# Score products on 64 lanes: two heads side by side instead of a stacked 128-lane product, with four score banks, one result bank and row groups of two and four

## The chip, the cores and the metric

One core of a Trainium2 chip runs the whole program. The metric is the device time of one execution in microseconds (us), lower is better.

## The reference

Two attentions follow each other, for batch 4, 768 rows and heads of 64. The first has 8 heads; each row sees the 128 rows up to itself and the first four rows (sinks). Its output x (768 x 512 a batch) goes into a mixture of 4 experts, each a causal attention of its own, of which every row takes two:

```python
keep = is_sink | in_window                       # first stage, 8 heads
x = softmax(where(keep, q @ k.T / 8, -1e9)) @ v  # -> (B, 768, 512)
logits = x @ w_gate                              # second stage, 4 experts
for e in range(4):
    a = softmax(where(causal, -1e9, (x @ wq[e]) @ (x @ wk[e]).T / 8))
    out += (top-2 weight of e) * (a @ (x @ wv[e]) @ wo[e])
```

## The kernel before

Heads go in pairs, since two heads of 64 fill the 128 lanes: four first-stage pairs a batch (`first`) and two second-stage pairs of experts (`second`), 24 units in all. A unit works through six blocks of 128 rows. Each block takes these steps:

- score products on PE into a PSUM bank `s` (L437);
- DVE adds the mask and takes the row's extreme (L638 in the first stage, L578 in the second);
- ACT takes the exponential and its sum (L643, L588);
- DVE and POOL make the factor and scale `p` (L477, L478, L668, L595; in the first stage POOL also merges two blocks, L661);
- PE transposes `p` into `t` (L495, L519), ACT or DVE copies that to `pt` (L339, L341);
- PE multiplies `pt` with the values into a result bank `acc` (L470), each head into its own 64 columns of the array ("cols").

After three blocks the result is read twice, by ACT (L322, high part) and then DVE (L327, low part), into `x` or `y`. Numbers are kept as a high and a low part, so that a product is three: high-high, high-low, low-high. The second stage makes its values (`values`, L772) and its queries and keys (L746) from `x`, and the output (`store`, L817) from `y`.

Score products stand in two forms. In batch 0 the first stage is **flat**: queries and keys hold high and low parts of both heads on 128 lanes, a head on 64 lanes each; three products, head by head alternating, on 64 rows of the array ("rows"). Everywhere else they are **stacked**: the low part of a head is moved by a DMA (L423) into the 64 lanes of the other head, below the high part, so that one 128-lane product with `ks` makes two of the three, and a second one with `kz` (half of it zeros, set once at L274) the third. For that ACT writes the high part twice (L400, 768 columns), DVE writes the low part to `ql` or `kl` (L404), and SyncE issues six DMAs a pair.

The order of work is made by a planner, `Plan`. Each step has a priority (its due time), a cost per engine and the steps and buffers that it waits for. `emit` takes, again and again, the step that can start first, the lower priority first among equals; on PE a step in another mode than the last (full height, "rows", "cols") counts as `STAY` later. A ring gives the number of buffers of a tile: three `s`, three `t`, two `acc`, together the eight PSUM banks. The units follow the list at L832 and L833: in each batch two first-stage pairs, both second-stage pairs of the batch before ("p"), two first-stage pairs.

Of the kernel before, what the change touches and what calls it, by code (L numbers as in the profile page):

```python
# [26 lines left out]
SWITCH = {("full", "cols"): 105, ("cols", "full"): 150, ("full", "rows"): 236, ("cols", "rows"): 236,  # L27
          ("rows", "full"): 90, ("rows", "cols"): 90}

STAY = 9.08  # L30
# [31 lines left out]
class Plan:  # L62
# [7 lines left out]
    def step(self, prio, cost, fn, after=(), new=(), use=(), fifo=None, moves=0, mode="full", behind=()):  # L70
        after = list(after)
        if fifo is not None:
            if fifo in self.fifo:
                after.append(self.fifo[fifo])
        s = Step(prio, cost, fn, after, new, use, moves, mode, behind)
        if fifo is not None:
            self.fifo[fifo] = s
        self.steps.append(s)
        return s

    def emit(self):
        free = {PE: 2000.0, DVE: 5000.0, ACT: 2000.0, POOL: 9500.0, SP: 650.0}
# [63 lines left out]
def kernel(  # L146
# [38 lines left out]
    pools = {tag: ctx.enter_context(tc.tile_pool(name=tag + "_", bufs=n, **(  # L185
        {"space": bass.MemoryType.PSUM} if tag in ("s", "t", "acc") else {}))) for tag, n in rings.items() if tag not in ("kz", "st", "psk", "vs")}
# [84 lines left out]
    kz = [consts.tile([128, 2, NB * SW], F32R, name=f"kz{n}") for n in range(rings["kz"])]  # L271
    for t in kz:
        for e in range(2):
            nc.vector.memset(t[64 - e * 64:128 - e * 64, e, :].bitcast(F32), 0.0)  # L274
    zeroed = itertools.cycle(kz)


    W, W_READY = {}, {}

    def weight(name, n, pieces, prio):  # L280
        cols = (EP if name == "wo" else NCH) * n
        st = buf("v2", [128, NB * E * D])
# [4 lines left out]
        def load():  # L287
            for sl, src in pieces:
                nc.sync.dma_start(sl(st.t[:, :cols].rearrange("p (c n) -> p c n", n=n)), src)

        ld = plan.step(prio, {SP: 460 * len(pieces)}, load, new=[st], fifo="v2", moves=730 * len(pieces))
        W_READY[name] = []
        for a in range(0, cols, 260):
            cs = slice(a, min(a + 260, cols))
            h = plan.step(prio + 3, {ACT: 320}, lambda cs=cs: nc.scalar.activation(hi[:, cs], st.t[:, cs], AF.Copy),
                          after=[ld], use=[st])
            W_READY[name].append(plan.step(
                prio + 3, {POOL: 695},
                lambda cs=cs: nc.gpsimd.tensor_sub(lo[:, cs], st.t[:, cs], hi[:, cs].bitcast(F32)),
                after=[h], use=[st]))  # L300

    def expert_pieces(w):
        return [((lambda t, e=e: t[:, :, e * D:(e + 1) * D]), w[e].rearrange("(c p) d -> p c d", p=128))
                for e in range(E)]
# [40 lines left out]
    class Pair:  # L345


        def __init__(self, ext, flat=False):
            self.ext, self.flat = ext, flat
            self.kw = SW if ext else 128  # L350
            self.n = NB * self.kw - (4 if ext else 0)
            self.qs, self.ks = buf("qs", [128, 2, S], F32R), buf("ks", [128, 2, NB * SW], F32R)
            if not flat:
                self.ql, self.kl = buf("ql", [128, S], F32R), buf("kl", [128, NB * SW], F32R)
                self.kz = Buf("kz", lambda: next(zeroed))
            self.splits = {0: [], 1: []}
            self.ready = {0: [], 1: []}

        def tiles(self, which):
            if self.flat:  # L360
                return [self.ks if which else self.qs]
            return [self.ks, self.kl, self.kz] if which else [self.qs, self.ql]

        def put(self, which, g, ps, t, prio, mul, after):
            use = [t, *self.tiles(which)]
            high, low = [], []  # L370
            w = NB * self.kw
            if which == 0:
                cs = slice(g * 384, g * 384 + 384)
                if self.flat:
                    high.append((ps, lambda: self.qs.t[:, 0, cs]))
                else:
                    high.append((lambda: ps()[:, None, :].to_broadcast([128, 2, 384]), lambda: self.qs.t[:, :, cs]))
                low.append((ps, lambda: self.qs.t[:, 0, cs], lambda: self.qs.t[:, 1, cs] if self.flat else self.ql.t[:, cs]))
            else:
                for sinks in range(2 if self.ext and g == 0 else 1):  # L380
                    js, cs = (slice(0, NB - 1), slice(128, SW)) if sinks else (slice(3 * g, 3 * g + 3), slice(0, 128))

                    def src(sinks=sinks):
                        x = ps()
                        return (x[:, None, :4].to_broadcast([128, NB - 1, 4]) if sinks
                                else x.rearrange("p (j c) -> p j c", c=128))

                    def at(x, js=js, cs=cs):
                        return x.rearrange("p (j c) -> p j c", c=self.kw)[:, js, cs]
                    if self.flat or sinks:  # L390
                        high += [(src, lambda e=e, at=at: at(self.ks.t[:, e, :w])) for e in range(1 if self.flat else 2)]
                    else:
                        high.append((lambda src=src: src()[:, None].to_broadcast([128, 2, 3, 128]),
                                     lambda js=js, cs=cs: self.ks.t[:, :, :w].rearrange("p e (j c) -> p e j c", c=self.kw)[:, :, js, cs]))
                    low.append((src, lambda at=at: at(self.ks.t[:, 0, :w]),
                                lambda at=at: at(self.ks.t[:, 1, :w] if self.flat else self.kl.t[:, :w])))

            def act():
                for src, dst in high:
                    nc.scalar.activation(dst(), src(), AF.Copy, scale=mul)  # L400

            def dve():
                for src, hi, dst in low:
                    nc.vector.scalar_tensor_tensor(dst(), src(), mul, hi().bitcast(F32), op0=OP.mult, op1=OP.subtract)  # L404
            some = 70 if self.ext and which and g == 0 else 0
            h = plan.step(prio, {ACT: some + 380 if self.flat else 2 * some + 690}, act, after, (), use)
            lo = plan.step(prio, {DVE: some * 1.3 + 470}, dve, [h], (), use)
            self.splits[which] += [h, lo]
            if g and not self.flat:
                self.stack(which, prio)  # L410

        def stack(self, which, prio):
            n = self.n if which else S
            for e in range(2):
                s, o = slice(e * 64, e * 64 + 64), slice(64 - e * 64, 128 - e * 64)
                if which:
                    moves = ((lambda e=e, o=o: self.ks.t[o, e, :n], lambda e=e, s=s: self.ks.t[s, e, :n]),
                             (lambda e=e, s=s: self.kz.t[s, e, :n], lambda s=s: self.kl.t[s, :n]))
                else:
                    moves = ((lambda e=e, o=o: self.qs.t[o, e, :n], lambda s=s: self.ql.t[s, :n]),)  # L420
                for dst, src in moves:
                    def go(dst=dst, src=src):
                        nc.sync.dma_start(dst().bitcast(F32), src().bitcast(F32))  # L423
                    self.ready[which].append(plan.step(prio, {SP: 600}, go, self.splits[which], (), self.tiles(which),
                                                       moves=830))

        def scores(self, outs, i, ks):

            qs = slice(i * 128, i * 128 + 128)
            for n in range(3 if self.flat else 2):  # L430
                for o, e in outs:
                    if self.flat:
                        hs, (a, b) = slice(e * 64, e * 64 + 64), THREE[n]
                        lhs, rhs = self.qs.t[hs, a, qs], self.ks.t[hs, b, ks]
                    else:
# [467 lines left out]
```

## Time and profile before

| what | value |
|---|---|
| median of 3 runs | 457.13 us (457.12 to 459.96) |
| the profiled execution | 457.69 us, span 456.0 us, granted clock 0.996 |
| instructions | 11,781, of them 3,920 matmuls |
| DMA | 95,852 packets, 51.94 MB |

Times in a view of the trace are counted from the span's start. The rows of a timeline have start, length, engine, line, operation, tiles, the part of the array (64*128 is half of its rows, 128*64 half of its columns), and the shape; a matmul's end is modelled, and its start is measured. Idle time before an instruction stands in brackets, with what ended it.

### The profile page before, as it was taken

The page shows a single profiled execution, that of the slowest core. Times are in us where ns is not written, and L with a number is a line of the kernel's source. Part 1 is how long each engine was busy: PE and PEld are TensorE (multiplying, and loading weights), DVE is VectorE, ACT ScalarE, POOL GpSimd, SP SyncE. Part 2 cuts the span into 40 slices and gives each one's busy share as a digit, 9 for nine tenths or more (in the row PEclk, how much of TensorE's full clock was granted, in tenths as well). Part 3 has the DMA queues.
Part 4 walks back from the last instruction along what each step waited for, and adds up shares of the span by engine and source line. Part 5 has one row for each costly group of instructions (what it writes and reads, how often), then busy time and mean ns, then how long its engine had stood idle before and what let it go on. Part 6 is the DMA issues. An engine that isn't in the chain of part 4 may idle for free.

```text
span 456.0 us, 11781 instructions
## 1 busy us (share of the span) xinstructions
PE 440.7 (97%) x3920; PEld 390.3 (86%) x3920; DVE 330.3 (72%) x1309; ACT 316.7 (69%) x906; POOL 265.3 (58%) x469
## 2 busy tenths in 40 slices
PE   5998899999999999999999999999999999999996
PEld 4777689999978889999987888999997888998775
DVE  6788783776898786766788788558689875376773
ACT  4898895765798877836688879647589845257540
POOL 7799786545666477435556675363565842025660
PEclk9999899999999999999999999999999999999999
DMA  8997895314466966402477579321413520404012
GB/s 173 199 197 149 208 198 108 81 36 104 85 147 157 220 182 159 106 15 57 105 175 162 130 190 237 73 52 36 105 37 74 128 94 25 105 2 104 2 47 92
DMA packets 95852, 51.94 MB, mean 114 GB/s; under 512 B 84784, under 2 KB 84784, under 8 KB 95792
## 3 DMA queue, kind: packets, MB, share of 16 engines
q1 hardware_dynamic: 95792, 51.19, 48.3%
q8 instruction: 31, 0.51, 0.5%
q14 instruction: 29, 0.24, 0.2%
HBM read 21.05 MB, written 6.29 MB: 60 GB/s over the span
## 4 chain that ended last, share of the span: by engine, by line
PE 81%; ACT 10%; DVE 3%; POOL 2%; issue 2%; DMA 0%; ACTq 0%; POOLq 0%; DVEq 0%
PE acc L470 19%; PE s L437 17%; PE t L746 15%; PE t L495 10%; PE t L772 7%; PE t L817 7%; PE t L720 3%; ACT p L643 2%; ACT pt L339 2%; PE t L519 2%; ACT p L588 2%; ACT ks L400 2%; ACT qs L400 2%; DVE pt L522 1%; PE t L525 1%
## 5 line engine op out<-in xcount | busy, mean ns | idle before, releaser
L437 PE MATMUL s<-ks,qs 64*128 64x260 f32 (+6 forms) x416 | 108.8, 346 | 1.8 <-DVE st L578 0.8
L643 ACT ACTIVATE p<-p,st 128x260 f32<-128x260 f32 (+1 forms) x192 | 93.4, 493 | 10.0 <-DVE st L638 8.7
L668 POOL TENSOR_TENSOR p<-p,st 128x256 f32<-128x256 f32 x96 | 65.5, 686 | 43.2 <-DVE st L478 33.2
L595 POOL TENSOR_TENSOR p<-p,st 128x128 f32<-128x128 f32 (+5 forms) x96 | 87.6, 933 | 3.8
L588 ACT ACTIVATE p<-p,st 128x256 f32<-128x256 f32 (+5 forms) x96 | 64.1, 670 | 28.5 <-DVE st L578 23.8
L638 DVE CUSTOM_DVE_ANT_0 p<-s,bmask 128x260 f32<-128x260 f32 (+1 forms) x192 | 72.2, 399 | 10.9 <-PE s L437 9.4
L437 PEld LDWEIGHTS s<-ks,qs 128*128 128x128 f32 (+1 forms) x416 | 64.5, 198 | 17.3 <-issue 7.1
L339 ACT ACTIVATE pt<-t 128x512 f32<-128x512 f32 (+1 forms) x109 | 57.6, 530 | 30.6 <-PE t L495 21.9
L437 PE MATMUL s<-kz,qs 128*128 128x260 f32 (+4 forms) x272 | 78.3, 304 | 0.0
L495 PE MATMUL t<-ident,p 128*128 128x128 f32 x432 | 63.1, 278 | 2.9 <-ACT qs L400 1.3
L661 POOL TENSOR_TENSOR p<-p 128x256 f32<-128x256 f32 x64 | 46.9, 733 | 18.2 <-ACT p L643 14.5
L495 PEld LDWEIGHTS t<-ident,p 128*128 128x128 f32 x432 | 48.9, 141 | 9.6 <-issue 2.8
L400 ACT ACTIVATE ks<-t 128x768 fp32r<-128x768 f32 (+2 forms) x76 | 38.8, 554 | 23.3 <-PE t L746 16.5
L481 POOL TENSOR_TENSOR st<-st,gate 128x2 f32<-128x2 f32 x48 | 9.4, 195 | 76.8 <-DVE st L478 62.3
L578 DVE CUSTOM_DVE_ANT_0 p<-s,cmask 128x512 f32<-128x512 f32 (+3 forms) x96 | 52.0, 551 | 1.1 <-PE s L437 0.8
L437 PEld LDWEIGHTS s<-kz,qs 128*128 128x128 f32 x272 | 51.6, 190 | 1.4
L400 ACT ACTIVATE qs<-t 128x768 fp32r<-128x768 f32 (+1 forms) x48 | 36.4, 759 | 13.6 <-PE t L746 10.3
L470 PE MATMUL acc<-pt,v 128*64 128x128 f32 x672 | 43.6, 277 | 0.4
L470 PEld LDWEIGHTS acc<-pt,v 128*64 128x64 f32 x672 | 36.0, 137 | 6.7 <-issue 2.6
L470 PE MATMUL acc<-pt,vn 128*64 128x128 f32 x448 | 40.3, 283 | 1.0 <-ACT pt L339 0.8
L618 POOL TENSOR_TENSOR dv<-vn 128x256 f32<-128x256 f32 x32 | 22.8, 731 | 29.9 <-PE acc L470 29.9
L341 DVE COPY pt<-t 128x512 f32<-128x512 f32 (+1 forms) x51 | 33.0, 647 | 9.7 <-PE t L495 9.1
(101 smaller groups left out, 959.6 us busy)
## 6 DMA issues: line engine op xcount, KB each, us to landing
qs<-ql SPq DMA_DIRECT2D x40, 192.0 KB, 3.1
vn<-in_v_dram SPq DMA_DIRECT2D x32, 192.0 KB, 3.4
out_dram<-o SPq DMA_DIRECT2D x24, 256.0 KB, 3.8
qn<-in_q_dram SPq DMA_DIRECT2D x30, 192.0 KB, 3.6
kn<-in_k_dram SPq DMA_DIRECT2D x30, 192.0 KB, 3.9
ks<-ks SPq DMA_DIRECT2D x24, 197.0 KB, 4.1
kz<-kl SPq DMA_DIRECT2D x24, 197.0 KB, 4.2
ks<-ks SPq DMA_DIRECT2D x16, 192.0 KB, 3.4
```

The lines of the kernel that those rows point to most:

```text
L339: nc.scalar.activation(dst(), src(), AF.Copy)
L400: nc.scalar.activation(dst(), src(), AF.Copy, scale=mul)
L437: nc.tensor.matmul(o, lhs, rhs, start=n == 0, stop=n == (2 if self.flat else 1))
L470: nc.tensor.matmul(o if e is None else o[e * 64:e * 64 + 64], lhs, rhs, start=first and e is not None, stop=last and i % 3 == 2)
L495: nc.tensor.transpose(t.t[:, 2 * e + c, :], block(e, c), ident)
L578: nc.vector.tensor_tensor_reduce(out=p.t[:, cs], in0=s.t[:, :(c1 - c0) * 128], in1=mask[:, cs], scale=1.0, scalar=st.t[:, 3, es] if c0 els ...
L588: nc.scalar.activation(x, x, AF.Exp, bias=st.t[:, 0, es], scale=-1.0, accum_out=st.t[:, 1, es])
L595: nc.gpsimd.tensor_mul(x, x, st.t[:, 2, e:e + 1].to_broadcast([128, n * 128]))
L638: nc.vector.tensor_tensor_reduce(out=p.t[:, e, a:], in0=s.t[:, a:RW], in1=row_mask[i][:, a:], scale=1.0, scalar=BIG, op0=OP.add, op1=OP.mi ...
L643: nc.scalar.activation(x, x, AF.Exp, bias=st.t[:, 0, e:e + 1], scale=-1.0, accum_out=st.t[:, 1, e:e + 1])
L668: nc.gpsimd.tensor_mul(x, x, st.t[:, 2, :][:, :, None].to_broadcast([128, 2, z - a]))
L746: nc.tensor.matmul(ps, w[a][:, c, es], X[b, c].t[:, x, cs], start=c == 0 and n == 0, stop=c == NCH - 1 and n == 2)
```

## The change

All score products become flat, in both stages: six matmuls a step, the two heads in turn. `ql`, `kl`, `kz`, the double write on ACT, the zeroing and all stacking DMAs go. A step takes two score banks at once, one a head; the ring `s` grows from three to four and `acc` shrinks from two to one. The row blocks of a unit form the groups 0-1 and 2-5 in place of 0-2 and 3-5: a group's result is one read of 256 or 512 columns, the second stage's queries and keys are made by group, and its steps wait only for the group they need. `wo` is loaded in two pieces into the ring `o` in place of one into `v2`. The planner's constants are new, among them the due times of the weights (`WP`, `WS`: from 7 to 15 apart), and so is the order of units: in a batch 0, 1, p0, 2, p1, 3, in the last 0, 1, 2, p0, 3, p1, c0, c1. The list is now kept in priority order per ring (`fifo`). Code for parts of batch 0 is there but off (`PARTS = 0`).

```diff
-STAY = 9.08
+STAY = 15.87
-    rings = {"qn": 2, "kn": 2, "vn": 3, "ql": 1, "kl": 1, "qs": 2, "ks": 2, "kz": 2, "x": 6,
-             "v2": 1, "y0": 1, "y1": 1, "p": 6, "dv": 2, "pt": 6, "psk": 4, "sk": 2, "vs": 2, "o": 2,
-             "gate": 2, "gates": 1, "st": 6, "s": 3, "t": 3, "acc": 2}
+    rings = {"qn": 2, "kn": 2, "vn": 3, "qs": 3, "ks": 3, "x": 6,
+             "v2": 1, "y0": 1, "y1": 1, "p": 8, "dv": 2, "pt": 6, "psk": 4, "sk": 2, "vs": 2, "o": 2,
+             "gate": 2, "gates": 1, "st": 6, "s": 4, "t": 3, "acc": 1}
...
-        def stack(self, which, prio):
...
-                    def go(dst=dst, src=src):
-                        nc.sync.dma_start(dst().bitcast(F32), src().bitcast(F32))
...
-            for n in range(3 if self.flat else 2):
-                for o, e in outs:
-                    if self.flat:
-                        hs, (a, b) = slice(e * 64, e * 64 + 64), THREE[n]
-                        lhs, rhs = self.qs.t[hs, a, qs], self.ks.t[hs, b, ks]
-                    else:
-                        lhs, rhs = self.qs.t[:, e, qs], (self.kz if n else self.ks).t[:, e, ks]
-                    nc.tensor.matmul(o, lhs, rhs, start=n == 0, stop=n == (2 if self.flat else 1))
+            for n, (a, b) in enumerate(THREE):
+                for e, o in enumerate(outs):
+                    hs = slice(e * 64, e * 64 + 64)
+                    nc.tensor.matmul(o, self.qs.t[hs, a, qs], self.ks.t[hs, b, ks], start=n == 0, stop=n == 2)
...
-            for heads in pair.heads():
-                for c0 in range(0, n, 4):
-                    c1 = min(c0 + 4, n)
-                    ss = {e: buf("s", [128, 512]) for e in heads}
+            for c0 in range(0, n, 4):
+                c1 = min(c0 + 4, n)
+                ss = [buf("s", [128, 512]) for _ in range(2)]
...
-            for g in range(2):
-                cs = slice(g * 384, g * 384 + 384)
+            for lo, hi in groups:
+                cs, n = slice(lo * 128, hi * 128), (hi - lo) * 128
...
-    ORD = "0 1 p0 p1 2 3"
-    LAST = "0 1 p0 p1 2 3 c0 c1"
+    CUTS_0, CUTS_N = "0 2 6", "0 2 6"
...
+    ORD = "0 1 p0 2 p1 3"
+    LAST = "0 1 2 p0 3 p1 c0 c1"
-    WP, WS = 2.88, 7.16
+    WP, WS, LOAD_0, PREP_3, VALUES_0 = 6.25, 14.87, 16.82, 11.14, 16.87
```

Three places on PE show how the order changes. The first is in the last two units of the program, where the score steps of a second-stage pair (s<-ks,qs) stand between transposes (t<-ident,p) and result products (acc<-pt,v). Before:

```order
L495 MATMUL t<-ident,p 128x128 x10
L470 MATMUL acc<-pt,v_6219 64x128 x10
L437 MATMUL s<-ks,qs 128x384
L437 MATMUL s<-kz_207,qs 128x384
L495 MATMUL t<-ident,p 128x128 x14
L470 MATMUL acc<-pt,v_6219 64x128 x14
L437 MATMUL s<-ks,qs 128x512
```

and now (line 416 is the score product, 466 the transpose, 437 the result product):

```order
L437 MATMUL acc<-pt,v_6295 64x128 x14
L466 MATMUL t<-ident,p 128x128 x10
L416 MATMUL s<-ks,qs 128x384 x6
L466 MATMUL t<-ident,p 128x128 x12
L437 MATMUL acc<-pt,v_6295 64x128 x22
L416 MATMUL s<-ks,qs 128x512 x12
L466 MATMUL t<-ident,p 128x128 x12
```

A head's two stacked products could stand alone, in the same mode as the transposes; now a step is six products of both heads in a mode of its own, often two steps together (x12).

The second place is the change from one result bank to the next, in the last unit. Before (the numbers are those of the tiles):

```order
L470 MATMUL acc_6564<-pt_6645,v2_6219 64x128 x4
L470 MATMUL acc_6564<-pt_6652,v2_6219 64x128 x4
L470 MATMUL acc_6564<-pt_6660,v2_6219 64x128 x4
L470 MATMUL acc_6689<-pt_6667,v2_6219 64x128 x2
L437 MATMUL s_6695<-ks_6409,qs_6328 128x512
```

and now, where the row of x4 is the last product of one result and the row of x6 begins the next:

```order
L437 MATMUL acc<-pt,v_6295 64x128 x4
L416 MATMUL s<-ks,qs 128x512 x6
L416 MATMUL s<-ks,qs 128x256 x6
L437 MATMUL acc<-pt,v_6295 64x128 x6
L805 MATMUL t<-woh,y_6584 128x512
```

Before, the next result began right behind the last, in the other bank; now other work stands between them while the one bank is read.

The third place is the end of the program, from the last transposes on. Before:

```order
L470 MATMUL acc<-pt,v_6219 64x128 x8
L495 MATMUL t<-ident,p 128x128 x14
L470 MATMUL acc<-pt,v_6219 64x128 x14
L817 MATMUL t<-woh,y_6524 128x512
L817 MATMUL t<-wol,y_6524 128x512
```

and now:

```order
L437 MATMUL acc<-pt,v_6295 64x128 x10
L466 MATMUL t<-ident,p 128x128 x12
L437 MATMUL acc<-pt,v_6295 64x128 x12
L805 MATMUL t<-woh,y_6584 128x512
L805 MATMUL t<-wol,y_6584 128x512
```

In both, four stores follow the last result product. Before, the first of the four is row block 2, of the group 0-2; now all four are of the group 2-5.

More of the change, by code (lines that the diff above doesn't have):

```diff
@@ L81, in emit @@
     def emit(self):
+        for line in self.fifo.values():
+            line.sort(key=lambda s: s.prio)
+            for a, b in zip(line, line[1:]):
+                if a not in b.after:
+                    b.after.append(a)
+                    a.then.append(b)
+                    b.waiting += 1
         free = {PE: 2000.0, DVE: 5000.0, ACT: 2000.0, POOL: 9500.0, SP: 650.0}
@@ L455, in mode, with fresh, tile, k_at @@
-        def mode(self):
-            return "rows" if self.flat else "full"
+        def fresh(self, which):
+            return ([], [self.tile(which)]) if self.ready[which] else ([self.tile(which)], [])
+        def tile(self, which):
+            return self.ks if which else self.qs
+        def k_at(self, x, js, cs):
+            x = x[..., :self.nk * self.kw]
+            return x.rearrange("p (j c) -> p j c" if len(x.shape) == 2 else "p e (j c) -> p e j c", c=self.kw)[
+                ..., js.start - self.k0:js.stop - self.k0, cs]
@@ L458, with score_cost, __init__ @@
+    def score_cost(n):
+        return 22 + 3 * max(109, n / 2.4 + 14)
     class Acc:
-        def __init__(self):
+        def __init__(self, lo, hi):
             self.b = buf("acc", [128, 512])
+            self.lo, self.hi = lo, hi
             self.begun, self.steps = set(), []
         def add(self, i, e, lhs, rhs, last=False):
-            o = self.b.t[:, (i % 3) * 128:(i % 3) * 128 + 128]
-            first = e not in self.begun
+            o = self.b.t[:, (i - self.lo) * 128:(i - self.lo) * 128 + 128]
+            nc.tensor.matmul(o[e * 64:e * 64 + 64], lhs, rhs, start=e not in self.begun, stop=last and i == self.hi - 1)
@@ L469, in add, with bufs @@
             self.begun.add(e)
-            nc.tensor.matmul(o if e is None else o[e * 64:e * 64 + 64], lhs, rhs,
-                             start=first and e is not None, stop=last and i % 3 == 2)
+        def bufs(self):
+            return ([], [self.b]) if self.steps else ([self.b], [])
     def factor(prio, st, after, weight=None, weight_after=()):
@@ L528, in av @@
         def av():
-            for r, acc in enumerate(accs):
+            for r in range(2):
                 for c in range(3):
@@ L535, in av, with wide_rows @@
                             acc.add(i + r, e, diff[0](i + r, e) if c else value[0](i + r - 1, e), (part if c else whole).t[:, r, e, :])
-        new = [] if accs[1].steps else [accs[1].b]
-        both = list({id(x): x for x in accs}.values())
-        s = plan.step(prio + AV_LAG, {PE: 1308}, av, [moved, tri, moved_sk, made_vs] + value[1] + diff[1], new,
-                      [whole, part, sk, vs] + value[2] + diff[2] + [acc.b for acc in both if acc.b not in new],
-                      fifo="av", mode="cols")
-        for acc in both:
-            acc.steps.append(s)
-    def wide_rows(prio0, step, pair, blocks, masks, value, weights, finish):
-        acc = None
+        new, used = acc.bufs()
+        acc.steps.append(plan.step(prio + AV_LAG, {PE: 1308}, av, [moved, tri, moved_sk, made_vs] + value[1](None) + diff[1], new,
+                                   [whole, part, sk, vs] + value[2] + diff[2] + used, fifo="av", mode="cols"))
+    def wide_rows(prio_of, pair, blocks, masks, value, weights, finish, groups):
         for i in range(NB):
-            if i % 3 == 0:
-                acc = Acc()
-            prio = prio0 + step * i
+            lo, hi = next(g for g in groups if g[0] <= i < g[1])
+            if i == lo:
+                acc = Acc(lo, hi)
+            prio = prio_of(i)
             cols, mask = blocks[i], masks[i]
@@ L591, in wide_rows, with exp @@
+            for e in range(2):
+                def exp(p=ps[e], es=slice(e, e + 1), n=n, st=st):
+                    x = p.t[:, :n * 128]
+                    nc.scalar.activation(x, x, AF.Exp, bias=st.t[:, 0, es], scale=-1.0, accum_out=st.t[:, 1, es])
+                sums.append(plan.step(prio - WIDE_E, {ACT: 278 + 0.833 * 128 * n}, exp, prev[e], (), [ps[e], st]))
+            r = factor(prio - WIDE_N, st, sums, weights and (lambda i=i: weights[0](i)), weights and weights[1][i])
             normed = []
@@ L694, in finisher, with over @@
-        return finish
-    def first(b, hp, prio0, step, prep_prio, load_prio):
+            n, cs = (acc.hi - acc.lo) * 128, slice(acc.lo * 128, acc.hi * 128)
+            ready[key].append((acc.lo, acc.hi, split(
+                prio, lambda: acc.b.t[:, :n], lambda: x.t[:, 0, cs], lambda: x.t[:, 1, cs], n, acc.steps,
+                [acc.b] + ([] if new else [x]), new=[x] if new else [], fifo=tag if new else None)))
+        return finish
+    def over(ready, lo, hi):
+        return [x for a, b, steps in ready if a < hi and b > lo for x in steps]
@@ L725, in first, with load @@
-        value = [lambda j, e: nat[2].t[:, j, e, :], loaded[2][:1], [nat[2]]]
+            j0 = pair.k0 if which else lo
+            parts = [(lo, 3), (3, hi)] if whole and which < 2 else [(j0, hi)]
+            loaded.append([])
+            for n, (a, z) in enumerate(parts):
+                def load(t=t, src=src, a=a, z=z, j0=j0):
+                    for e in range(2):
+                        nc.sync.dma_start(t.t[:, a - j0:z - j0, e, :],
+                                          src[b, 2 * hp + e].rearrange("(t p) d -> p t d", p=128)[:, a:z, :])
+                before = [x[2][0] for x in loaded[-1]]
+                loaded[-1].append((a, z, [plan.step(
+                    load_prio + (0.1 if n else 0.2 if which == 2 else 0), {SP: 950}, load, (), [] if n else [t], [t] if n else [],
+                    moves=364 * (z - a), behind=before, fifo=None if n else tag)]))
@@ L734, in second @@
+    def second(b, ep, groups, prio_of, prep_of):
         pair = Pair(False)
@@ new lines, in mm @@
+                    def mm(c=c, ps=ps, qs=qs):
+                        for n, (a, w) in enumerate(THREE):
+                            nc.tensor.matmul(ps()[:, :VW], X[b, c].t[:, a, qs], W["wv"][w][:, c, :],
+                                             start=c == 0 and n == 0, stop=c == NCH - 1 and n == 2)
+                    last = plan.step(prio, {PE: 360}, mm,
+                                     [last] + [r for cc in range(NCH) for r in over(X_READY[b, cc], i, i + 1)] + W_READY["wv"],
+                                     ([t] + ([v2] if i == 0 else [])) if c == 0 else [],
+                                     [X[b, c]] + ([t] if c else []) + ([v2] if i else []), fifo="v2" if c == 0 and i == 0 else None)
@@ L860 @@
         if kind == 0:
             f = firsts.index(u)
-            first(b, n, place[u], 10.0 / NB, place[u] - (PREP_1 if b else PREP_0),
-                  -100.0 if f == 0 else place[firsts[f - 1]] - PREP_1)
-        else:
+            first(b, n, cuts[b] if g is None else [cuts[b][g]], at_row(b, n, 0, 10.0), place[u] - (PREP_1 if b else PREP_0),
+                  -100.0 if f == 0 else place[u] - LOAD_0 if b == 0 else place[firsts[f - 1]] - PREP_1,
+                  None if g is None else keys[n])
+        elif (b, n) not in done and all(x in place and units.index(x) <= units.index(u) for x in units if x[0] == b and not x[2]):
+            done.add((b, n))
+            row = at_row(b, n, 1, 20.0)
```

541 lines of the change are left out of this document (258 added, 283 removed).

## The prediction

> **What bounds the kernel now.** I read the page's first part and the chain, then the windows, then the timeline of PE.
>
> ```profile
> span 456.0 us, 11781 instructions
> PE 440.7 (97%) x3920; PEld 390.3 (86%) x3920; DVE 330.3 (72%) x1309; ACT 316.7 (69%) x906; POOL 265.3 (58%) x469
> PE 81%; ACT 10%; DVE 3%; POOL 2%; issue 2%; DMA 0%; ACTq 0%; POOLq 0%; DVEq 0%
> ```
>
> PE sets the time: 97% busy, 81% of the chain. But the ends of its records are modelled, so I price a matmul by the distance to the next start, not by its record.
>
> ```profile
> 3.95 0.87 PE L720 MATMUL t<-ident,qn 128*128 128x128 f32 x3 [3.95 <-POOL bmask L204]
> 66.00 0.28 PE L772 MATMUL t<-wvh,x 128*128 128x260 f32 x1
> 446.70 0.40 PE L817 MATMUL t<-wol,y 128*128 128x512 f32 x1
> 446.93 0.62 PE L817 MATMUL t<-woh,y 128*128 128x512 f32 x2
> 447.39 0.39 PE L817 MATMUL t<-wol,y 128*128 128x512 f32 x1
> 142.20 0.28 PE L437 MATMUL s<-ks,qs 128*128 128x260 f32 x1
> 142.32 0.28 PE L437 MATMUL s<-kz,qs 128*128 128x260 f32 x1
> 142.44 0.28 PE L437 MATMUL s<-ks,qs 128*128 128x260 f32 x1
> 428.94 0.40 PE L437 MATMUL s<-ks,qs 128*128 128x512 f32 x1
> 429.17 0.40 PE L437 MATMUL s<-kz,qs 128*128 128x512 f32 x1
> 429.41 0.40 PE L437 MATMUL s<-ks,qs 128*128 128x512 f32 x1
> 22.64 0.63 PE L437 MATMUL s<-ks,qs 64*128 64x260 f32 x6
> 23.20 0.33 PE L525 MATMUL t<-ident,psk 128*128 128x128 f32 x1
> 23.36 0.60 PE L519 MATMUL t<-ident,p 128*128 128x128 f32 x4
> 23.89 0.63 PE L437 MATMUL s<-ks,qs 64*128 64x260 f32 x6
> 125.55 1.75 PE L470 MATMUL acc<-pt,v 128*64 128x128 f32 x28
> 127.23 0.50 PE L437 MATMUL s<-ks,qs 128*128 128x512 f32 x1
> ```
>
> A full-height score matmul costs 0.12 us at 260 columns and 0.235 at 512. On 64 lanes (64*128 rows, used before only in batch 0), six matmuls cost 22.64 to 23.20 = 0.56 us: two heads run side by side, so they are three steps of 0.12, and 0.20 is left over for going into the mode and coming out. The five transposes between two such runs take 23.20 to 23.89 = 0.69, which is 5 x 0.11 and 0.14 over. The 28 column matmuls (14 pairs of 0.109) take 1.68, 0.15 over. So **each change of mode costs**: 0.20 us for a run of rows, 0.15 of columns, 0.14 of full height.
>
> Priced this way, the 3,920 records stream for 393.7 us; the order of PE has 161 runs of one mode (22 rows, 63 columns, 76 full), worth 24.6. X
>
> ```profile
> 12.00:66.00 54.00, 50.46 (x488) 39.62 (x487) 43.38 (x195) 48.94 (x164) 48.77 (x85) 0.97 0.94 188
> 66.00:120.00 54.00, 53.87 (x482) 50.93 (x481) 36.12 (x148) 35.30 (x101) 31.06 (x54) 1.00 0.39 87
> 120.00:140.00 20.00, 19.17 (x172) 15.95 (x173) 18.01 (x67) 17.98 (x45) 11.66 (x19) 1.00 0.66 150
> 200.00:220.00 20.00, 20.00 (x182) 18.80 (x181) 14.85 (x56) 13.22 (x33) 8.75 (x16) 1.00 0.27 61
> ```
>
> Columns after the length: PE, PEld, DVE, ACT, POOL busy, clock, DMA share. Up to 66 us ACT (48.9 of 54) and POOL (48.8) set the pace. Later PE does, but for a stretch in each batch such as 120 to 140, where DVE and ACT have 18 of 20 us; by my prices some 2 us are lost in each of 130-140, 240-250 and 350-360, and none at 200-220.
>
> **The change, part by part.** *Scores.* 136 of the 160 score steps (two heads, one row block) leave the full-height form:
>
> ```profile
> L437 PE MATMUL s<-ks,qs 128*128 128x260 f32 x120 | 37.7, 331 | 0.7 <-DVE st L578 0.6
> L437 PE MATMUL s<-ks,qs 128*128 128x512 f32 x48 | 21.9, 456 | 0.2 <-DVE st L578 0.2
> L437 PE MATMUL s<-ks,qs 128*128 128x128 f32 x56 | 15.0, 280 | 0.0
> L437 PE MATMUL s<-ks,qs 128*128 128x256 f32 x32 | 9.9, 317 | 0.0
> L437 PE MATMUL s<-ks,qs 128*128 128x384 f32 x16 | 6.0, 376 | 0.0
> ```
>
> These are half of the matmuls (the other half reads kz), two to a step: 60 steps of 260 columns, 24 of 512, 28 of 128, 16 of 256, 8 of 384. A step was four matmuls and becomes three side-by-side pairs. Before: 60 x 0.48 + 24 x 0.94 + 28 x 0.45 + 16 x 0.47 + 8 x 0.70 = 77 us. After: three quarters, 58. **Streaming falls by 19.3 us.** Pairs of 384 and 512 columns are in no row of before. Bounds: as side by side as at 260 (no loss), or not at all (+21 us: 24 x 0.70 + 8 x 0.52). I take the first: two pairs of 260 already stream at the price of one.
>
> *Modes.* In the new order I count 84 runs of rows (74 of them two steps long), 71 of columns, 94 of full height: 62 x 0.20 + 8 x 0.15 + 18 x 0.14 = **+16.1 us**. Low end: a clean run of 128-column rows, 18.44 to 18.92 less 0.33, is 0.155; at that the sum is 12. High end 0.25, since 38 runs go straight from rows to columns, which no clean stretch shows: 20.
>
> ```profile
> 18.44 0.55 PE L437 MATMUL s<-ks,qs 64*128 64x128 f32 x6
> 18.92 0.33 PE L525 MATMUL t<-ident,psk 128*128 128x128 f32 x1
> ```
>
> So PE's work falls by only **3.2 us** (-7 to +1). Most of what the pairs save is paid back in changes of mode.
>
> Here the Trainium skill speaks against the change. "TensorE: Matmul & The Clock Gate", section LDWEIGHTS (loading the stationary operand), gives columns / 1.2 ns for a weight load whatever its rows: 107 ns for 128 columns, half height or not, so by it alone six loads make a step of 0.64 us, as an estimate. The row at 22.64 has the whole run of six, both ends included, in 0.56, so the trace does not bear that out; Part 3 of the same page lets loads of different row groups overlap.
>
> *Copies and stacks.* 80 copies of 768 columns on ACT become 384 (the row of batch 0):
>
> ```profile
> L400 ACT ACTIVATE qs<-t 128x768 fp32r<-128x768 f32 x40 | 32.5, 814 | 10.3 <-PE t L746 10.3
> L400 ACT ACTIVATE qs<-t 128x384 fp32r<-128x384 f32 x8 | 3.9, 486 | 3.2 <-PE t L720 3.2
> 136.87 0.52 PE L495 MATMUL t<-ident,p 128*128 128x128 f32 x3 [0.45 <-ACT qs L400]
> qs<-ql SPq DMA_DIRECT2D x40, 192.0 KB, 3.1
> ```
>
> That is 80 x 0.33 = 26 us off ACT, and PE's wait at 136.87 is for just such a copy, in the stretch that loses 2 us. The two second-stage units of a batch also no longer stand next to each other, so DVE's work (unchanged) comes more evenly. Of the 6 us in the three stretches I take **-4** (-6 to 0, since DVE at 18 of 20 us may hold PE by itself). The 120 stacking DMAs (40 qs, 40 ks, 40 kz) and the memsets of kz are hidden behind work begun well ahead: 0 when they go.
>
> *Up to 66 us.* ACT saves 8 copies of batch 1's first two pairs (2.6 us). POOL's splits of wk and wo (2.79 us each, the second in the chain of waits) move later; the value products of rows 0-1 may begin before the last rows of batch 0 are done. Against that: POOL and DVE keep nearly all their work. **-2** (-5 to +2).
>
> ```profile
> 63.02 2.79 POOL wol L299 x4
> 47.68 2.79 POOL L299 TENSOR_TENSOR wkl<-v,wkh 128x260 fp32r<-128x260 f32 x4 [1.40 <-ACT wkh L295]
> L322 ACT ACTIVATE x<-acc 128x384 fp32r<-128x384 f32 x32 | 15.5, 486 | 4.2 <-PE acc L470 3.9
> L327 DVE SCALAR_TENSOR_TENSOR x<-acc,x 128x384 fp32r<-128x384 f32 x32 | 17.7, 554 | 7.2 <-ACT x L322 7.0
> ```
>
> *One result bank.* The first product of a new group must now wait until ACT and then DVE have read the old one: 0.49 + 0.55 at 384 columns, some 1.3 with the hops; 0.2 more at 512 (by the columns). Behind it in PE's queue stands everything. There are 47 hand-overs; the new order puts 1.4 to 21 us of other PE work into them by my prices, 13 of them under 2.2. Were each reading to take 2.0 us, 1.5 us would stay uncovered; at 2.2, 3; at 2.7, 10 (18 gaps too short). I take **+1.5** (0 to +10).
>
> *The end.* Of the four stores behind the last product (L817, six matmuls of 0.23, 1.4 us each), the first needed only the group before and covered the reading. Now all four need the group 2-5: the reading lies bare, **+1.5** (1 to 2).
>
> **Sum**, against the profiled execution's 457.69 us (span 456.0): 457.7 - 3.2 - 4 - 2 + 1.5 + 1.5 = **451.5 us**; the median shown, 457.13, is 0.6 under that execution.
>
> **Rivals.** *Even*: DVE holds PE in the same stretches, and the first 66 us keep their length: 457.7 - 3.2 + 1.5 + 1.5 = 457.5, inside 1%. For it: DVE's 18 of 20 us, with work that the change leaves. Against: the wait at 136.87 is ACT's. *Slower, by the result bank*: readings of 2.7 us, as when ACT and DVE have a queue; then +10, and with the stretches unrelieved 457.7 - 3.2 + 10 + 1.5 = 466. It decides from about 2.4 us a reading, where shortfalls pass 5 us. For it: 18 short gaps. Against: 1.04 us of the two reads themselves, and ACT has less to do. *Half-height loads in a row*: if each of six loads took the 0.11 us at which 128-column matmuls follow each other, a step would cost at least 0.66; steps of up to 260 columns rise by 0.30 or so, 104 x 0.30 = 31 us: 482. The 0.56 of a whole run speaks against it. (It is the rule above as a mechanism.) *Much faster*: the waits of the stretches and half of those before 66 us go, and rows cost 0.155: 457.7 - 7 - 6 - 7 + 3 = 441. For it: 26 us less ACT work where ACT is at 90%. Against: POOL at 90% there too. *It does not do what it says*: no; the order has no stack and six matmuls in every score step.
>
> **How the numbers follow.** About 1% (4.6 us) is what a measurement of this kernel can tell from no change: below 452.6 is faster, above 461.7 slower. Forecast 0.42 (own range 447 to 456), even 0.28, slower by the bank 0.14, serial loads 0.03, much faster 0.13. The forecast's own range lies about four fifths below 452.6. Faster: 0.34 + 0.13 = 0.47; slower: 0.12 + 0.03 + 0.01 = 0.16; same: 0.37. The range 442 to 463 leaves out part of both ends.
>
> **What would show it.** In the profile after: six 64*128 rows of 512 columns in about 0.70 us between starts; runs of rows with 0.20 over; ACT busy near 290 us; copies of 384; no qs<-ql DMA; PE idle before its first products on ACT x or DVE x lines under 3 us in all; a gap of about 1.5 us before the last four stores. I am wrong if 512-column pairs take more than 0.25 us each, if rows cost well over 0.20 a run, or if PE waits for the result bank or for DVE by 5 us more than before.

## The result, and the profile after

The changed kernel takes 444.55 us (median of four, 444.12 to 445.26) against 457.28 of the kernel before: a ratio of 0.971, 95% interval 0.968 to 0.974. The forecast was 451.5. The direction was right, but the gain of 12.7 us is more than twice the 5.8 forecast.

The page of the changed kernel, first part and the chain:

```profile
span 443.1 us, 12131 instructions
PE 431.0 (97%) x4192; PEld 361.5 (82%) x4192; DVE 322.0 (73%) x1302; ACT 291.2 (66%) x897; POOL 264.8 (60%) x469
PE 80%; DVE 9%; ACT 6%; issue 3%; DMA 1%; POOL 1%; SPq 0%; ACTq 0%; DVEq 0%
```

PE is still 97% busy, and ACT has 291 us in place of 317. The share tells nothing of what was gained, so I split the time as the prediction did. **PE's work** is every matmul at its price (0.109 us for 128 columns, 0.117 for 256, 0.119 for 260, 0.175 for 384, 0.231 for 512, half of that for one on half of the array) and, for every run of one mode, the price of changing into it and out (0.20 for rows, 0.15 for columns, 0.14 for full height). What the starts in the trace have beyond that are **PE's waits**. One table serves all runs (work and waits are of the profiled execution):

| kernel | median us | PE's work | waits up to 66 us | waits after |
|---|---|---|---|---|
| before | 457.3 | 418.0 | 15.0 | 15.2 |
| **after** | **444.6** | **415.0** | **11.5** | **9.0** |
| after, old order of units | 452.6 | 417.9 | 11.7 | 14.6 |
| after, double copies on ACT | 452.1 | 415.0 | 12.5 | 15.1 |
| after, both of these and two qs, ks | 460.0 | 417.4 | 13.5 | 20.5 |
| after, two qs, ks alone | 450.0 | 416.8 | 11.2 | 13.0 (3.4 of it a slower clock) |
| after, groups 0-3 and 4-5 | 452.8 | 416.8 | 12.2 | 13.0 |
| after, weights as early as before | 448.4 | 415.6 | 14.3 | 9.4 |
| after, 128-lane products | 449.5 | 415.4 | 10.2 | 14.1 |
| after, three score and two result banks | 480.0 | 431.8 | 12.6 | 26.9 (some 5 of it a slower clock) |
| after, modes not held | 468.7 | 436.7 | 13.5 | 9.6 |
| after, heads one after the other | 445.0 | 415.0 | 11.4 | 9.3 |
| after, numbers moved 3%, two draws | 448.8, 447.7 | 416.4, 416.7 | 12.5, 13.0 | 10.5, 8.4 |
| before, all products flat | 502.5 | 434.5 | 15.8 | 44.1 (some 3 of it a slower clock) |
| before, single copies on ACT | 459.8 | 418.2 | 15.7 | 17.3 |
| before, new order of units | 476.1 | 420.9 | 14.8 | 30.2 |
| before, both of these | 472.0 | 419.9 | 15.9 | 27.1 |
| before, numbers moved 3%, two draws | 465.6, 456.8 | 420.1, 417.2 | 14.3, 15.3 | 21.1, 16.0 |

PE's work fell by 3.0 and the waits by 9.7, together 12.7 of the 12.9 by which the span fell; the rest lies ahead of PE's first product (at 3.95 us before, 3.67 now). The products are as forecast. A stretch of PE's timeline, where the first x12 row is a step of 512 columns and one of 128, the second one of 512 and one of 256:

```profile
201.94 0.39 PE L437 MATMUL acc<-sk,vs 128*64 128x128 f32 x4
202.26 1.25 PE L416 MATMUL s<-ks,qs 64*128 64x512 f32 x12
203.44 0.65 PE L466 MATMUL t<-ident,p 128*128 128x128 f32 x4
...
206.11 0.88 PE L437 MATMUL acc<-pt,v 128*64 128x128 f32 x12
206.91 1.32 PE L416 MATMUL s<-ks,qs 64*128 64x512 f32 x12
208.17 1.10 PE L466 MATMUL t<-ident,p 128*128 128x128 f32 x8
```

From 206.91 to 208.17 are 1.26 us: three pairs at 0.231, three at 0.117 and 0.2 for the mode. Pairs of 512 columns run side by side at about the price of one full-height product (0.231), straight out of the column mode too. By the Trainium skill ("TensorE: Matmul & The Clock Gate", LDWEIGHTS, 107 ns a load of 128 columns) twelve loads one after the other would take at least 1.28 us, as an estimate; the run at 202.26 takes 1.18, mode change included, so the trace does not agree.

PE's waits after 70 us, first before, then after:

```profile
PE t L495 <- ACT qs L400: 1.3, 3, 0.4
PE s L437 <- DVE st L578: 0.8, 4, 0.2
PE t L495 <- DVE pt L522: 0.3, 2, 0.2
```

```profile
PE acc L437 <- ACT pt L340: 0.8, 1, 0.8
PE s L416 <- DVE st L543: 0.6, 1, 0.6
PE t L805 <- DVE pt L493: 0.3, 2, 0.2
```

(The view counts a wait only from the modelled end of the matmul ahead, so it names the culprits but not the size.) The waits for ACT's double copy are gone; the copies themselves are these now:

```profile
L388 ACT ACTIVATE qs<-t 128x384 fp32r<-128x384 f32 x32 | 15.8, 492 | 4.0 <-PE t L703 4.0
L388 ACT ACTIVATE qs<-t 128x512 fp32r<-128x512 f32 x8 | 4.8, 594 | 9.8 <-PE t L731 9.8
L388 ACT ACTIVATE qs<-t 128x256 fp32r<-128x256 f32 x8 | 3.0, 380 | 3.5 <-PE t L731 3.5
```

The end, from the last result products on:

```profile
431.50 1.58 PE L437 MATMUL acc<-pt,v 128*64 128x128 f32 x24
433.01 0.50 PE L805 MATMUL t<-woh,y 128*128 128x512 f32 x1
433.35 0.39 PE L805 MATMUL t<-wol,y 128*128 128x512 f32 x1
433.58 0.69 PE L805 MATMUL t<-woh,y 128*128 128x512 f32 x2
434.11 0.40 PE L805 MATMUL t<-wol,y 128*128 128x512 f32 x1
434.50 0.73 PE L805 MATMUL t<-woh,y 128*128 128x512 f32 x2
```

ACT and DVE read the bank behind those products:

```profile
433.13 0.60 ACT L323 ACTIVATE y<-acc 128x512 fp32r<-128x512 f32 x1 [1.36 <-PE acc L437]
433.76 0.69 DVE L328 SCALAR_TENSOR_TENSOR y<-acc,y 128x512 fp32r<-128x512 f32 x1 [1.39 <-ACT y L323]
```

The first store starts right behind the products, before ACT has read: its three matmuls of the first pair need only the `y` of the other unit. The reading of the bank costs some 0.3 us in small gaps, not 1.5. Nor does the bank hold PE elsewhere: the median reading took 1.51 us from the last product's modelled end, and after 70 us no wait of PE stands against it in the view.

### The profile page after: what moved, and what is told of

It reads as the page before. It is cut to its first block, busy times and chain, and to the rows that moved or that the text cites. A ratio compares the mean times of both kernels' runs of the same rounds, so it can differ in the third digit from the quotient of the medians.

```text
span 443.1 us, 12131 instructions
## 1 busy us (share of the span) xinstructions
PE 431.0 (97%) x4192; PEld 361.5 (82%) x4192; DVE 322.0 (73%) x1302; ACT 291.2 (66%) x897; POOL 264.8 (60%) x469
## 4 chain that ended last, share of the span: by engine, by line
PE 80%; DVE 9%; ACT 6%; issue 3%; DMA 1%; POOL 1%; SPq 0%; ACTq 0%; DVEq 0%
PE acc L437 18%; PE s L416 15%; PE t L731 15%; PE t L466 11%; PE t L759 8%; PE t L805 6%; PE t L703 4%; PE t L490 2%; ACT pt L340 2%; DVE p L607 2%; DVE pt L493 2%; ACT p L553 2%; DVE p L543 1%; DVE qs L392 1%; ACT p L612 1%
## 5 line engine op out<-in xcount | busy, mean ns | idle before, releaser
L416 PE MATMUL s<-ks,qs 64*128 64x260 f32 (+4 forms) x960 | 92.8, 322 | 0.6 <-DVE st L543 0.6
L416 PEld LDWEIGHTS s<-ks,qs 64*128 64x128 f32 x960 | 69.2, 190 | 19.4 <-issue 10.1
L637 POOL TENSOR_TENSOR p<-p,st 128x256 f32<-128x256 f32 x96 | 65.9, 690 | 27.1 <-DVE st L449 14.6
L553 ACT ACTIVATE p<-p,st 128x128 f32<-128x128 f32 (+5 forms) x96 | 63.8, 668 | 14.4 <-DVE st L543 12.4
L607 DVE CUSTOM_DVE_ANT_0 p<-s,bmask 128x260 f32<-128x260 f32 (+1 forms) x192 | 68.8, 400 | 3.6 <-PE s L416 2.8
L543 DVE CUSTOM_DVE_ANT_0 p<-s,cmask 128x512 f32<-128x512 f32 (+3 forms) x96 | 50.1, 552 | 4.5 <-PE s L416 4.4
L448 DVE TENSOR_REDUCE st<-st 128x2 f32<-128x4 f32 x144 | 22.2, 154 | 23.1 <-ACT p L612 11.9
L388 ACT ACTIVATE ks<-t 128x384 fp32r<-128x384 f32 (+3 forms) x64 | 24.8, 416 | 20.0 <-PE t L731 17.4
L759 PE MATMUL t<-wvh,x 128*128 128x260 f32 x192 | 37.0, 288 | 0.4 <-ACT pt L340 0.4
L612 ACT ACTIVATION_READ_ACCUMULATOR p<-p,st 128x1 f32 x192 | 37.1, 193 | 0.0
L805 PE MATMUL t<-woh,y 128*128 128x512 f32 x96 | 35.2, 414 | 0.3 <-DVE pt L493 0.3
```

Source lines behind the costliest of these rows:

```text
L416: nc.tensor.matmul(o, self.qs.t[hs, a, qs], self.ks.t[hs, b, ks], start=n == 0, stop=n == 2)
L553: nc.scalar.activation(x, x, AF.Exp, bias=st.t[:, 0, es], scale=-1.0, accum_out=st.t[:, 1, es])
L607: nc.vector.tensor_tensor_reduce(out=p.t[:, e, a:], in0=s.t[:, a:RW], in1=row_mask[i][:, a:], scale=1.0, scalar=BIG, op0=OP.add, op1=OP.mi ...
L612: nc.scalar.activation(x, x, AF.Exp, bias=st.t[:, 0, e:e + 1], scale=-1.0, accum_out=st.t[:, 1, e:e + 1])
L637: nc.gpsimd.tensor_mul(x, x, st.t[:, 2, :][:, :, None].to_broadcast([128, 2, z - a]))
L759: nc.tensor.matmul(ps()[:, :VW], X[b, c].t[:, a, qs], W["wv"][w][:, c, :], start=c == 0 and n == 0, stop=c == NCH - 1 and n == 2)
```

## The experiments

Theory: ACT's halved copies took the waits away. Rivals: the order of units, the row groups, the banks, the later weights. The ratios are to the kernel before, with 95% intervals.

**Four runs on the copies, the order and the flat form.** Double copies again (`a_twice`); `both` broadcasts the source into both halves of the tile, and DVE overwrites the second as ever:

```diff
-                for src, dst in pieces:
+                for src, dst in pieces if self.once else pieces[1:]:
                     nc.scalar.activation(dst(0), src(), AF.Copy, scale=mul)
+                if not self.once:
+                    src, dst = both()
+                    nc.scalar.activation(dst, src, AF.Copy, scale=mul)
```

> The changed kernel with ACT writing each high part twice again outside the first stage of batch 0 (768 columns a copy in place of 384; DVE then overwrites the second half as ever, so nothing is left out). 26 us more on ACT, the order of all instructions unchanged. Theory (ACT's relief): waits come back, 450 to 453. Rival (order of units, groups, banks): under 1 us, 445.

The old order of units (`a_units`):

```diff
-    ORD = "0 1 p0 2 p1 3"
-    LAST = "0 1 2 p0 3 p1 c0 c1"
+    ORD = "0 1 p0 p1 2 3"
+    LAST = "0 1 p0 p1 2 3 c0 c1"
```

> The changed kernel with the old order of units (0 1 p0 p1 2 3). PE's order then has 268 runs of one mode in place of 249, +2.9 us. Theory (ACT's relief): only that, 447.5. Rival (the evener order of units took the three stretches' waits away): +2.9 + 6 = 453.5.

452.05 (ratio to before 0.987, 0.985 to 0.989) and 452.56 (0.989, 0.986 to 0.991): theory and rival are both right. The copies bring 6.1 us of waits back after 66 us, the old order 5.6 and 2.9 of modes. Both runs keep the changed kernel's due times, and with double copies the planner still reckons with short ones: each number is the worth of the part within a plan that was made for it, and no run has due times made anew without the part. The windows of 230 to 340 us, after and then with double copies, show it: ACT (fourth) goes from 74.3 to 81.1 us of 110, and PE (first) gets through 1,023 matmuls in place of 1,072.

```profile
230.00:340.00 110.00, 108.03 (x1072) 90.55 (x1068) 83.83 (x336) 74.32 (x228) 63.20 (x106) 1.00 0.20 48
```

```profile
230.00:340.00 110.00, 105.84 (x1023) 87.67 (x1023) 82.78 (x331) 81.09 (x225) 63.37 (x108) 1.00 0.19 48
```

Single copies in the kernel before (`b_half`), and all its products flat (`b_flat`):

```diff
-                    high.append((lambda: ps()[:, None, :].to_broadcast([128, 2, 384]), lambda: self.qs.t[:, :, cs]))
+                    high.append((ps, lambda: self.qs.t[:, 0, cs]))
...
-        pair = Pair(banded, flat=b == 0)
+        pair = Pair(banded, flat=True)
```

> The kernel before, with ACT writing each high part once (384 columns) in place of twice; the second halves are filled by the same DMAs with the low part, so part of each score product is left out of the result. PE's order stays nearly the same (161 runs and one more). Theory (ACT's 26 us of copies made the waits): 457.3 - 6 = 451 to 452. Rival (order of units, groups, banks): 457, within 1 us.

> The kernel before with all its score products on 64 lanes (its own flat form, until now only in batch 0): no stacks, no double copies on ACT, but three score banks, two result banks, groups of three and the old order of units. By the prices of the prediction PE streams 19.0 us less, but with three banks two steps seldom stand together: 358 runs of one mode in place of 161, 35.5 us more. Theory (ACT's halved copies are what took the waits away): 457.3 + 16.5 - 6 = 468. Rival (the waits went with the order of units, the groups or the fourth score bank): 457.3 + 16.5 = 474.

459.84 (1.005, 1.004 to 1.006): nothing gained, against the theory, and 2 to 3 us over the rival's 457. And 502.51 (1.096, 1.091 to 1.101): the flat form alone is a large loss, 28 us over even the rival's 474, and so far beyond the 16.5 us that streaming and modes add. Its waits name DVE above all; the two rows of `s` are PE waiting for DVE to empty the three score banks, of which a step takes two:

```profile
PE s L437 <- DVE st L638: 4.2, 8, 0.8
PE t L495 <- DVE qs L404: 4.2, 3, 1.4
...
PE acc L470 <- DVE pt L341: 3.6, 5, 0.8
PE s L437 <- DVE st L578: 3.4, 7, 0.7
```

**Banks, form, turn of the heads.** The changed kernel with the banks of before (`a_acc2`), with four products of 128 lanes a step (`a_tall`), with the loop over the heads outside (`a_serial`); and the kernel before with the new order of units (`b_units`, the lists above):

```diff
-             "gate": 2, "gates": 1, "st": 6, "s": 4, "t": 3, "acc": 1}
+             "gate": 2, "gates": 1, "st": 6, "s": 3, "t": 3, "acc": 2}
```

```diff
-            for n, (a, b) in enumerate(THREE):
-                for e, o in enumerate(outs):
-                    hs = slice(e * 64, e * 64 + 64)
-                    nc.tensor.matmul(o, self.qs.t[hs, a, qs], self.ks.t[hs, b, ks], start=n == 0, stop=n == 2)
+            for e, o in enumerate(outs):
+                for n in range(2):
+                    nc.tensor.matmul(o, self.qs.t[:, e, qs], self.ks.t[:, n, ks], start=n == 0, stop=n == 1)
```

```diff
-            for n, (a, b) in enumerate(THREE):
-                for e, o in enumerate(outs):
+            for e, o in enumerate(outs):
+                for n, (a, b) in enumerate(THREE):
```

> The changed kernel with the banks of before: three score banks, two result banks. A score step takes two banks, so two steps can no longer stand together: PE's order has 341 runs of one mode in place of 249, +16.8 us. Theory (the bank count, not the old order or the groups of three, made the all-flat kernel before so slow; its waits were 60 us in place of 30): 444.6 + 16.8 + 30 = 491. Rival (the modes alone): 461.

> The changed kernel with each score step as four products of 128 lanes in place of six of 64: no mode of its own, nothing stacked, so every score mixes both heads (the result is not the reference's). PE streams 21.8 us more and has 133 runs of one mode in place of 249, 21.4 us less. If the prediction's sum for the products is right (what the pairs save goes into changes of mode): 445, within 1.5. Rival (side-by-side products are themselves what gained): 450 or more.

> The changed kernel with the heads not alternating: three products of one head, then three of the other; the same matmuls in the same steps. If two products stream side by side only when neighbours stand on different halves: four of the six no longer pair, about two thirds of 58 us more, 480 to 485; if none pairs, 503. Rival (the pairing does not hang on the order): 445.

> The kernel before with the new order of units (0 1 p0 2 p1 3). PE's order has 181 runs of one mode in place of 161, +2.9 us. Theory A (the even order by itself takes the waits of the three stretches away): 457.3 + 2.9 - 5 = 455. Theory B (it needs ACT's relief as well, since the changed kernel loses 7 us with either of the two taken back): 459 to 461.

Three score banks: 479.99 (1.046, 1.041 to 1.052; 475.5 in the one run at full clock), between the 461 of the modes alone and the theory's 491. A fourth score bank in place of the second result bank is worth over 30 us: 16.8 of modes and the rest waits. The result bank that paid for it cost nearly nothing, by the trace above. The 128-lane products: 449.47 (0.981, 0.978 to 0.984). Work is equal to 0.4 us as forecast, but the time is 4.9 us longer and not within 1.5: the waits after 66 us are 5.1 more, those before 1.3 fewer. Why was not settled, so it stays open whether the pairs also gain by something else than PE's work. The heads one after the other: 445.0 in a single run, within the spread of the changed kernel (last section). The new order in the kernel before: 476.12 (1.041, 1.037 to 1.045), 15 us over even theory B: both theories are wrong.

**Tiles, groups, weights, modes**, one line each (`a_ring2`, `a_cut46`, `a_weights`, `a_stay0`):

```diff
-    rings = {"qn": 2, "kn": 2, "vn": 3, "qs": 3, "ks": 3, "x": 6,
+    rings = {"qn": 2, "kn": 2, "vn": 3, "qs": 2, "ks": 2, "x": 6,
...
-    CUTS_0, CUTS_N = "0 2 6", "0 2 6"
+    CUTS_0, CUTS_N = "0 4 6", "0 4 6"
...
-    WP, WS, LOAD_0, PREP_3, VALUES_0 = 6.25, 14.87, 16.82, 11.14, 16.87
+    WP, WS, LOAD_0, PREP_3, VALUES_0 = 2.88, 7.16, 16.82, 11.14, 16.87
...
-STAY = 15.87
+STAY = 0.0
```

> The changed kernel with two qs and two ks tiles, as before, in place of three (the third has the room of ql, kl and kz). PE's order has 260 runs of one mode in place of 249, +1.8 us. Theory (the even order of units lets queries and keys be made ahead only with a third tile, which is why the order alone cost the old kernel 18 us): waits come back, 452 to 460. Rival (the third tile is idle): 446.4.

> The changed kernel with the row groups 0-3 and 4-5 in place of 0-1 and 2-5. PE's order has 261 runs in place of 249, +1.8 us. Theory (a first group of two rows lets the values begin early, and that took 3.9 us of waits away before 66 us): the first value product comes later than 59.5 us and the time is 444.6 + 1.8 + 4 = 450. Rival (the later weights did it): 446.4.

> The changed kernel with the old due times of the weights (2.88 and 7.16 apart in place of 6.25 and 14.87). PE's order has 252 runs, +0.6 us. Theory (the row groups took the waits before 66 us away): 445. Rival (the later weights, which put ACT's and POOL's splits behind the rows, did it): 445 + 4 = 449.

> The changed kernel with a planner that does not hold a mode (STAY 0 in place of 15.87): 382 runs of one mode in place of 249, by 0.20, 0.15 and 0.14 us a run 21.7 us more, streaming the same. If those prices are right and the waits stay: 466. If a change of mode costs nothing: 445. More waits would come on top, less is possible only by what the planner gains by its free choice, under 5.

Two tiles gave 449.99 (0.981, 0.975 to 0.986), but the granted clock (last but two) fell in the profiled run:

```profile
300.00:320.00 20.00, 19.14 (x174) 15.71 (x172) 15.99 (x65) 13.22 (x44) 10.06 (x21) 1.00 0.00 1
320.00:340.00 20.00, 19.16 (x148) 16.20 (x148) 9.65 (x36) 9.58 (x23) 9.74 (x12) 0.83 0.01 2
```

That stretch alone costs 3.4 us; the one run at full clock took 446.81. So, by that run, the rival holds: the third tile is all but idle. The groups: 452.81 (0.989, 0.985 to 0.993). The first value product came later, at 61.4 us, as the theory has it; but the waits grew by 4.0 us after 66 us and by only 0.7 before, so the groups are worth something, though not for the reason I gave. The weights: 448.36 (0.980, 0.977 to 0.983): the rival holds, the later weights took 2.8 of the 3.5 us before 66 us away. In the window from 12 to 62 us PE got 2.8 us less done with early weights (first row) than after:

```profile
12.00:62.00 50.00, 45.85 (x475) 36.29 (x474) 43.30 (x195) 45.01 (x160) 46.94 (x83) 1.00 0.86 178
```

```profile
12.00:62.00 50.00, 48.62 (x508) 38.79 (x506) 44.09 (x200) 46.25 (x165) 46.45 (x81) 1.00 0.87 179
```

Modes not held: 468.72 (1.024, 1.021 to 1.028), +24.2, where the prices say 21.7 and 2.5 are left as waits. That fits the prices of the modes.

**Fit or room?** The parts' waits add up to more than the change won. Perhaps any other order loses a fit of the planner's numbers. So all lead and unit times were moved by 3%, two draws a kernel, such as:

```diff
-    LEAD_S, LEAD_E, LEAD_N = 8.54, 2.53, 4.23
+    LEAD_S, LEAD_E, LEAD_N = 8.80, 2.61, 4.10
```

> The changed kernel with its fourteen lead times, unit lengths and preparation times each moved by 3% up or down at random; nothing else changes. PE's order has 258 runs of one mode, +1.4 us. Theory F (the last 6 us of waits went because the planner's numbers fit just this order, and any other order loses them): waits after 66 us come back to 13 to 15, 450 to 452. Theory S (they went for good with three tiles, even order, less ACT and two-row groups): 446.

> As the last, with another draw of the 3%: 260 runs of one mode, +1.7 us. Theory F: 450 to 452. Theory S: 446.3.

> The kernel before with its own lead times, unit lengths and preparation times each moved by 3% at random: 175 runs of one mode in place of 161, +2.1 us. If the numbers of before fit its order as tightly as those of the changed kernel theirs: 457.5 + 2.1 + 4 or more = 463 or more. If its order had no such fit to lose: 459.6.

> As the last, with a draw that has fewer runs of one mode than before (155 in place of 161, -0.8 us). Tight fit: 461 or more. No fit: 456.7.

448.81 (0.980, 0.978 to 0.982) and 447.70 (0.977, 0.975 to 0.980) lie between the times of the two theories; their 10.5 and 8.4 us of waits after 66 go with theory S. Some 3 to 4 us of the result are fit (modes, and waits before 66 us), but the low waits later on are not, to 1.5 us. Two draws a kernel are few, and 3% does not test a plan made for another order. The kernel before gave 465.56 (1.017, 1.014 to 1.019) and 456.76 (0.998, 0.997 to 1.000): its waits scatter from 15 to 21, so `b_half`'s 17.3 can neither show nor exclude a few us from the copies there.

**Three parts taken back at once (`a_three`), and two put into the kernel before (`b_both`)**, with the edits above together:

> The changed kernel with three parts taken back at once: the old order of units, two qs and ks tiles, double copies on ACT. PE's order has 265 runs of one mode, +2.4 us. If what each part guards is the same room (waits after 66 us came back to 13 to 15 with any one of them taken back): waits near 16, 454. If each part carries its own waits, they add: 9 + 5.6 + 4.0 + 6.1 = 25 us, 463.

> The kernel before with both: ACT writing each high part once (part of each score product left out, as above) and the new order of units. PE's order has 174 runs of one mode in place of 161, +1.9 us. If the two parts work together in the old form as they do in the changed kernel (where they are worth 11.5 us of waits between them): waits under 30, 450 to 455. If the even order does not fit the old kernel's stacks and due times: 470 or more.

460.04 (1.004, 1.002 to 1.006): the flat form, four banks, new groups and new due times without the order and the copies' relief are no faster than the kernel before. The time lies between the two forecasts, nearer to the 463 of parts whose waits add than to the 454 of a shared room. The 25 us of that sum counted 4.0 for the third tile, of which 3.4 were a slower clock; without the tile it is 9.0 + 5.6 + 6.1 = 20.7, and 20.5 was measured. So they add. ACT's copies lead the list again, as before:

```profile
PE t L473 <- ACT qs L395: 1.5, 3, 0.7
```

472.03 (1.030, 1.026 to 1.033) in the old form, so the two parts do not work together there: the even order costs 18.8 us with the double copies and 12.2 with single ones (against `b_half`). Why was not settled: its due times were made for the old order, and its stacks need one `ql` and one `kl` for all pairs.

## Why the prediction was right in direction and too small

1. *Streaming and modes, -3.2*: right. 3.0 by the same prices, and `a_stay0` bears the prices of the modes out to 2.5 of 24.2 us. (The bounds of 12 and 20 for the modes come out as 13.3 and 19.2 by the prices named; the forecast does not hang on them.)
2. *Copies and order, -4 ("Of the 6 us in the three stretches I take -4")*: **a step that failed**, by 2.5 us (the waits after 66 us fell by 6.2 on balance, 6.5 with the 0.3 of the end). The two together are worth 11.5 us there, in a plan made for both. In the new kernel both parts do what the step says; the old kernel does not show it, and the bound was wrong: I capped the relief by the 6 us that the trace of before shows in three stretches. But without the relief the new form has 20.5 us there and not 15.2, so there was more to relieve than the old trace could show. (Whether the form itself adds those 5 us is not shown: the neighbours of the kernel before reach 21.) Counted at the same times, though other units now stand there, the three stretches fell from 5.7 to 0.6 us; the rest fell elsewhere, where I had put nothing.
3. *Up to 66 us, -2*: -3.5 measured, within its bounds. 2.8 of it came from the later weights (their splits on ACT and POOL, then the engines that set the pace), which I named; rows 0-1 going ahead brought 0.7 at most (by `a_cut46`): with early weights the first value product even came at 58.6 us, after at 59.5, before at 66.0. (The profiled run of before had a lower clock near 50 us, 0.97 in the window from 12 to 66, at most some 1.6 us; but executions of it at a clock of 1.0 took no less, 457.3 us and up.)
4. *One result bank, +1.5, and the end, +1.5*: **the other step that failed**, by 2.7 us: near 0 and 0.3. The +1.5 for the bank goes with readings of 2.0 us; they took 1.51, and the work between two results, 1.4 us and up by the prediction's own count, covered that. The +1.5 for the end overlooked that the first store begins with three matmuls of the other unit and goes on with two that need only ACT's half of the reading. That the readings cost nothing rests on the trace; no run had two result banks beside four score banks.
5. *Not in the sum at all*: that the fourth score bank decides. In place of a second result bank it is worth some 30 us; the modes I counted (74 runs of two steps) had it in silently.

The profiled execution fell by 12.9 us where the sum had 6.2. Of the 6.7 between them 2.7 are the hand-over and the end that did not come, 2.5 the relief and 1.5 the time up to 66 us; PE's work fell by 0.2 less than forecast, and its earlier first product makes up for that. That the products came out right is in part luck: their sum had the fourth bank's 16.8 us of modes in it without a word.

## What to carry to other kernels

What a relief is worth can't be capped by the waits in the old trace when the same change may add load: price the new form without the relief first. A form that saves streaming can lose more to changes of mode and to banks than it saves, so count runs of one mode in the new order and ask how many steps the banks let stand together. Test a part by taking it out of the new kernel, not only by putting it into the old one, and move the planner's numbers a little to see what is mere fit.

## What the runs showed of the hardware

Half-height products of two heads ran side by side in both orders tried: three of one head and then three of the other took as long as the six in turn, in one run. First the run with the heads one after the other, then the changed kernel, two steps of 260 columns each:

```profile
280.05 0.99 PE L416 MATMUL s<-ks,qs 64*128 64x260 f32 x12
```

```profile
279.96 0.98 PE L416 MATMUL s<-ks,qs 64*128 64x260 f32 x12
```

In the trace of the former the starts stand in pairs 0.010 us apart, in the latter 0.004; so, if the compiled program keeps the order of the source, which the trace does not print, the second head's first product starts ahead of the first head's second one. The Trainium skill ("TensorE: Matmul & The Clock Gate", Step-by-step: what each phase is for) has matmuls in program order, with weight loads alone pulled ahead; on that condition this run does not agree.
